# Attention with forgetting, then a SiLU feed-forward: turning the first blocks of batches four to seven with full-array products, and a new order of loads on SyncE

## The chip, the cores and the metric

The kernel runs on one core of a Trainium2 chip. The metric is the device time of one execution in microseconds (us), and less is better. TensorE (PE in the profile) multiplies matrices into PSUM, ScalarE (ACT) and VectorE (DVE) work on PSUM and SBUF, GpSimd (POOL) works on SBUF and issues DMAs, and SyncE (SP) issues DMAs. A number such as L298 is a line of the kernel before.

## The reference

Inputs are q, k, v of 8 batches x 8 heads x 576 tokens x 64, forget values f, and two weights. All are float32.

```python
scores = scale * q @ k.T                  # scale = 1/8
cum = cumsum(log(clip(f, 1e-4, 1)))
attn = softmax(where(causal, scores + cum[:, None] - cum[None, :], -1e9))
x = (attn @ v) laid out as 4608 tokens x 512
h = x @ w_in                              # 512 x 2048
out = (h * sigmoid(h)) @ w_out            # 2048 x 512
```

## The kernel before

**Tiling.** All matmuls take bf16. Each head's 576 tokens are a first block of 128, three more blocks of 128 ("the rest") and a tail of 64. The decay is split into a factor for each key, which is multiplied into v, so that the softmax needs no row maximum: exp of the scores, a mask, the product with v and a column of ones, and a division. Two heads make a pair; a unit n is one pair of one batch, b, p = divmod(n, 4), 32 units in all.

**Stages.** First come the first blocks of batches 0 to 3, in straight code (L780 to L821). Then `two_more(4, True)` (L883) and `two_more(6, False)` (L889) do the first blocks of batches 4, 5 and 6, 7. Then a loop over m (L965) takes two units at a time and computes the rest and the tails. The feed-forward runs in between: `m1_chunk` (L574) makes 128 columns of the hidden layer for a group of tokens (four matmuls into `hp`, a tanh on ACT, L589, a product on DVE, L590), and `m2_part` (L608) or `m2_rows` (L643) multiplies by `w_out`. `fill(us, least)` (L752) puts such steps between the attention's, by costs that are written in the code; it knows nothing of when a buffer is free.

**A first block.** `load_qk0(b)` (L129) brings q and k so that a partition holds eight neighbouring tokens of one head (16 such runs x 8 heads = 128 partitions), in `qkb`. The scores need them with the 64 features in the partitions. `turn0(b, i)` (L290, i = 0 for q, 1 for k) does this with matmuls against `sel` (L233): for each of the 8 tokens of a run, and for each of two sets of heads, one matmul of 128 rows x 64 columns against 64 columns, which lands in the upper or lower half of the partitions of one PSUM tile `tp` (L298). One copy of 128 x 512 then takes it to SBUF: q on ACT, k on DVE (L305). `scores0` (L322) multiplies the two (L332) and takes exp on ACT (L339), `mask0` (L346) masks on DVE where no ban was added beforehand (`ban0`, L310), `out0` (L362) multiplies by v and divides, `back0` (L395) turns the result with four products of 128 columns (L402) and copies it (L403) into the token group's tile. `two_more(b, ...)` turns q and k of batch b, puts a filling step, turns q and k of batch b + 1, puts a filling step, and goes on with the scores of the one and of the other.

**Buffers.** PSUM has two pools: `psc` (two tiles of two banks, for scores) and `pbig` (L69), four tiles of one bank each under one tag "big". `tp`, `hp`, `po`, `tx`, `dn` and `pr` all take turns in these four.

**Order.** The order on each engine is the order in the text (`manual_schedule`, L54); the framework sets the semaphores between engines from what the instructions read and write, and gives a tile a free buffer. DMAs issued on one engine wait in that engine's order too.

**Loads of the loop.** `turn(n)` (L895) casts the tail columns of unit n + 3 on POOL (`cast_qk`, L407) and issues its transposing DMA on SP (`transposes`, L437). `prepare(n)` (L900) issues the loads of later units: q and k of unit n + 4 on POOL (L160); at p = 2 the tails of batch b + 2 on SP (`load_tails`, L180); the v blocks of batch b + 1 (`load_v`, L192), on SP for batch 1 and on POOL from batch 2 on; and, at p = 2 and 3, the conversions of v on POOL (`convert_v`, L427). Now `prepare(n)` comes behind `turn(n)` (L986, L995, L1016).

Of the kernel before, what the change touches and what calls it, by code (L numbers as in the profile page):

```python
# [10 lines left out]
FP32 = mybir.dt.float32  # L11
BF16 = mybir.dt.bfloat16
P = 128
# [5 lines left out]
def kernel(  # L19
# [10 lines left out]
    nc = tc.nc  # L30

    B, H, S, D = q.shape
# [4 lines left out]
    NP = H // 2  # L37
# [7 lines left out]
    NU = B * NP  # L45
    NQ = NU // 2
    HD = D // 2
    RUN = 8
# [10 lines left out]
    qktp = ctx.enter_context(tc.tile_pool(name="qktp", bufs=4))  # L59
# [9 lines left out]
    pbig = ctx.enter_context(tc.tile_pool(name="pbig", bufs=4, space=bass.MemoryType.PSUM))  # L69
# [5 lines left out]
    sel = const.tile([P, 2, D], BF16, name="sel")  # L75
# [7 lines left out]
    kT0 = [const.tile([P, NP, P], BF16, name=f"kT0_{b}") for b in range(B)]  # L83
# [149 lines left out]
    for i in range(2):  # L233
        for g in range(2):
            nc.vector.tensor_copy(
                out=sel[:, i, :].rearrange("p (u w r) -> p u w r", u=2, w=2)[:, g, :, :],
                in_=ident_bf[:, :].rearrange("p (r u i w) -> p u i w r", u=2, i=2, w=2)[
                    :, g, i, :, :
                ],
            )  # L240

    def keep_warm(n):
# [7 lines left out]
        out=f_sb[:, :], in0=f_sb[:, :], scalar1=1e-4, scalar2=1.0, op0=ALU.max, op1=ALU.min  # L250
# [39 lines left out]
    def turn0(b, i):  # L290
        src = qk0[b]
        if i == 0:
            qT0[b] = qktp.tile([P, NP, P], BF16, name="qT0", tag="qT0", bufs=2)
        dst, evac = ((qT0[b], nc.scalar.copy), (kT0[b], nc.vector.tensor_copy))[i]
        tp = pbig.tile([P, NP, NRUN, RUN], FP32, name="tp", tag="big")
        for c in range(RUN):
            for j in range(2):
                nc.tensor.matmul(  # L298
                    tp[j * D : (j + 1) * D, :, :, c].rearrange("p a r -> p (a r)"),
                    lhsT=src[:, i, c * D : (c + 1) * D],  # L300
                    rhs=sel[:, j, :],
                    start=True,
                    stop=True,
                )
        evac(  # L305
            out=dst[:, :, :].rearrange("p a t -> p (a t)"),
            in_=tp[:, :, :, :].rearrange("p a r c -> p (a r c)"),
        )

    def ban0(b):  # L310
        sc = psc.tile([P, 2, NP, P], FP32, name="sc", tag="sc")
        for i in range(2):
            nc.tensor.matmul(  # L313
                sc[:, i, :, :].rearrange("p a t -> p (a t)"),
                lhsT=ident_bf[:, :],
                rhs=ban[:, :, :].rearrange("p a t -> p (a t)"),
                start=True,
                stop=False,
            )
        return sc  # L320
# [25 lines left out]
    def mask0(b):  # L346
        x = u0[b][:, :, :, :].rearrange("p i a t -> p (i a) t")
        nc.vector.tensor_tensor(
            out=x, in0=x, in1=tri[:, None, :].to_broadcast([P, H, P]), op=ALU.mult
        )  # L350
# [56 lines left out]
    def cast_qk(n):  # L407
        b, p = divmod(n, NP)
        if n < NP:
            qbf[n] = conv.tile([P, NX, 2 * D], BF16, name="qkb", tag="qkb")  # L410
        t2 = qbf[n]
        for i, t in enumerate(qst.pop(n) if n < NP else ()):
            c0 = i * (NR + 1)
            nc.gpsimd.tensor_copy(
                out=t2[:, c0 : c0 + NR, :].rearrange("p c x -> p (c x)"),
                in_=t[:, :, :, :].rearrange("p c h d -> p (c h d)"),
            )
        nc.gpsimd.tensor_copy(
            out=t2[:, NR, :].rearrange("s (i d) -> s i d", i=2),
            in_=tst[b].rearrange("s (u i w) d -> s u w i d", u=2, w=2)[:, p // 2, p % 2, :, :],  # L420
        )
# [15 lines left out]
    def transposes(n):  # L437
        src = qbf.pop(n)
        t = qktp.tile([P, NX, P], BF16, name="qkT", tag="qkT")
        qkT[n] = t[:, :, :].rearrange("p x c -> p (x c)")  # L440
        nc.sync.dma_start_transpose(
            out=t[:, :, :], in_=src[:, :, :].rearrange("p x c -> p (x c)")
        )
# [308 lines left out]
    def fill(us_, least=0, ends=(0, 0)):  # L752

        left = us_ + at["left"]
        kinds = plan(left)
        kinds += [0] * (least - len(kinds))
        if any(ends) and kinds:
            if 2 not in kinds:
                kinds[0] = 2
            n1, n2 = len(kinds) - kinds.count(2), kinds.count(2)  # L760
            e0 = 1 if ends[0] else 0
            e1 = 1 if ends[1] and n2 > e0 else 0
            inner = n2 - e0 - e1
            n = n1 + inner
            mid = [2 if (x + 1) * inner // n > x * inner // n else 1 for x in range(n)]
            if inner and mid[-1] == 2 and e1 and not e0:
                mid = mid[::-1]
            kinds = [2] * e0 + mid + [2] * e1
        for k in kinds:
            t = step(k)  # L770
            if t is None:
                at["left"] = 0.0
                return
            left -= t / 1000
        at["left"] = left
# [84 lines left out]

    def two_more(b, banned):
        for x in range(2):
            turn0(b + x, 0)
            turn0(b + x, 1)
            fill(0.6, 1)
        for x in range(2):
            if banned:
                scores0(b + x, ban0(b + x))
            else:
                scores0(b + x)  # L870
                mask0(b + x)
            fill(0.6 if x == 0 else 2.0 if banned else 2.8, 1 if x == 0 else 2)
        out0(b)
        fill(0.6, 1)
        out0(b + 1)
        fill(0.8, 2)
        back0(b, on_act)
        fill(0.6, 1)
        back0(b + 1, on_act)
        fill(0.6, 1)  # L880
# [14 lines left out]
    def turn(n):  # L895
        if n < NU - 3:
            cast_qk(n + 3)
            transposes(n + 3)

    def prepare(n):  # L900

        b, p = divmod(n, NP)
        if n != NP - 1 and n + 4 < NU:
            load_qk(n + 4)
        if b + 1 == B:
            return
        if p == 2 and b + 2 < B:
            load_tails(b + 2)
        if b == 0 and p >= 2 or b > 0 and p == 1:
            for c in range(NM) if b > 0 else range(2 * (p - 2), 2 * (p - 1)):  # L910
                load_v(b + 1, c)
        if n == NP - 1:
            load_qk(n + 4)
        if p >= 2:
            for c in range(2 * (p - 2), 2 * (p - 1)) if b > 0 else range(NM * (p - 2)):
                convert_v(b + 1, c)
# [48 lines left out]
    for m in range(NQ):  # L965
        n = 2 * m
        piece = 1.7 if m < 2 else 2.4
        if m == 2:
            assert at["m2"] >= M2_OF[0]
            first_pool.__exit__(None, None, None)  # L970
            gpools[0] = ctx.enter_context(tc.tile_pool(name="third", bufs=1))
            lag["g"] = 2
        if m == 4:
            lag["parts"] = 12
        goal = (spent() if m <= 4 else goal) + QUAD[m]
        rows = whole() if m > 0 and BY_DMA[m - 1] else None
        scores(n, 0)
        scores(n, 1)
        if m > 0:
            back(m - 1)  # L980
        turn(n)
        if m > 0:
            if m % 2 == 0:
                b = m // 2 - 1
                pending.append([2, [REST_OF[b]] + ([TAILS_OF[b][0]] if b == NM - 1 else [])])
        prepare(n)  # L986
        if rows:
            at["m2"] += 4
            m2_rows(*rows, 0)
            m2_fence(*rows)  # L990
            mask(n)
            scores(n, 2)
            scores(n + 1, 0)
            turn(n + 1)
            prepare(n + 1)  # L995
            m2_rows(*rows, 1)
            mask_tail(n)
            mask(n + 1)
            scores(n + 1, 1)
            scores(n + 1, 2)  # L1000
            m2_out(*rows)
            passed()
            attend(n)
            mask_tail(n + 1)
            slot(1.9, 3)
            attend(n + 1)
            slot(1.8)
            rest(goal)
            at["left"] = 0.0
            continue  # L1010
        slot(piece, 0, (1, 0))
        mask(n)
        scores(n, 2)
        scores(n + 1, 0)
        turn(n + 1)
        prepare(n + 1)  # L1016
        slot(piece, 0, (1, 0))
        mask_tail(n)
        mask(n + 1)
        scores(n + 1, 1)  # L1020
        scores(n + 1, 2)
        mask_tail(n + 1)
        slot(piece, 0, (1, 0))
        attend(n)
        attend(n + 1)
        slot(min(3.5, max(0.8, behind() - LAG)) if m > 1 else 0.8)
# [39 lines left out]
```

## Time and profile before

| | |
|---|---|
| three runs | 342.59 us median, 340.6 to 344.43 |
| the profiled execution | 340.25 us, span of its instructions 338.5 us |
| TensorE busy | 331.3 us, 4136 matmuls |
| L298, the turning matmuls | 256, from 5.5 to 48.8 us |
| L332 in the two stages of two_more | from 27.67 to 29.8 and from 49.98 to 51.25 us |
| 16 DMA engines | 52.4% of the span for POOL's queue, 43.2% for SP's |

How to read it: "busy" is the time in which an engine has work, "xN" a count of instructions, and the last figures of a group are the idle time ahead of it and who ended it. The chain of waits is followed from the last instruction backwards to what released it; its rows are start, length, engine, tile, line and count, in us. The timeline merges equal instructions; "PEld" is TensorE's load of weights, "SPq" the issue of a DMA on SP. The end of a matmul is modelled, so the start of the next is the better measure of its length.

### The profile page before, as it was taken

The numbers are of one execution on the slowest core, as the hardware profiler recorded it, in microseconds if no ns is written. First come the engines' busy times: TensorE is split into PE (matmuls) and PEld (weight loads), VectorE is DVE, ScalarE is ACT, GpSimd is POOL, SyncE is SP. The second block draws the span as 40 slices with busy tenths as digits, with TensorE's granted clock in tenths as the row PEclk, the third lists the DMA queues.
The fourth block names the chain that finished last, engine by engine and source line by source line (L and its number), as shares of the span: only waits on it lengthen the run. The fifth ranks groups of instructions, "written<-read, shape, count | busy, mean of one in ns | idle before, by whom it ended". The sixth has DMA issues, their size and how long they took to land.

```text
span 338.5 us, 10020 instructions
## 1 busy us (share of the span) xinstructions
PE 331.3 (98%) x4136; PEld 222.7 (66%) x4136; DVE 189.8 (56%) x423; ACT 216.9 (64%) x389; POOL 188.0 (56%) x269
## 2 busy tenths in 40 slices
PE   7999999999999999999999999999999999999995
PEld 3745655577656767858767796867777685555654
DVE  4665735265467458656665865675485564333330
ACT  5767735776767767848748794875877583344331
POOL 8995417893798998999995994694000000000000
PEclk9999999999999999999999999999999999999999
DMA  8999999999699999999999999896452200001012
GB/s 156 190 188 222 189 199 166 186 213 174 114 109 214 138 212 137 169 219 197 150 169 123 200 133 117 149 185 85 99 74 61 59 35 31 31 33 64 33 62 62
DMA packets 124542, 45.24 MB, mean 134 GB/s; under 512 B 111824, under 2 KB 118224, under 8 KB 124496
## 3 DMA queue, kind: packets, MB, share of 16 engines
q0 software_dynamic: 53536, 18.88, 52.4%
q1 hardware_dynamic: 70800, 25.59, 43.2%
q8 instruction: 32, 0.52, 0.7%
q10 hardware_dynamic: 160, 0.13, 0.2%
q14 instruction: 14, 0.11, 0.1%
HBM read 36.85 MB, written 9.44 MB: 137 GB/s over the span
## 4 chain that ended last, share of the span: by engine, by line
PE 93%; ACT 2%; DMA 1%; DVE 1%; issue 1%; POOL 0%; POOLq 0%
PE hp L581 36%; PE po L626 25%; PE pr L652 12%; PE sc L473 7%; PE dn L520 6%; PE dn L529 3%; PE tp L298 2%; DMA qkb<-in_k_dram 1%; PE sc L313 1%; PE sc L332 1%; DVE gt L590 1%; ACT x L403 1%; PE tx L562 1%; DVE xq L387 0%; ACT th L589 0%
## 5 line engine op out<-in xcount | busy, mean ns | idle before, releaser
L590 DVE SCALAR_TENSOR_TENSOR gt<-th,hp 128x384 bf16<-128x384 bf16 (+2 forms) x208 | 107.4, 523 | 74.6 <-ACT th L589 65.8
L589 ACT ACTIVATE th<-hp 128x384 bf16<-128x384 f32 (+2 forms) x208 | 96.5, 471 | 73.4 <-PE hp L581 71.7
L581 PE MATMUL hp<-x,w_in_bf 128*128 128x384 bf16 (+2 forms) x704 | 123.0, 321 | 0.5 <-DVE x L565 0.3
L581 PEld LDWEIGHTS <-w_in_bf 128*128 128x128 bf16 x832 | 78.9, 98 | 49.4 <-issue 1.1
L626 PE MATMUL po<-w_out_bf,gt 128*128 128x512 bf16 (+1 forms) x400 | 93.8, 371 | 0.0
L484 ACT ACTIVATE u<-sc 128x1024 bf16<-128x1024 f32 (+1 forms) x96 | 74.7, 817 | 7.0 <-PE sc L473 7.0
L626 PEld LDWEIGHTS <-gt 128*128 128x128 bf16 x400 | 37.6, 98 | 32.5 <-issue 0.2
L652 PE MATMUL pr<-w_out_bf,gt 64*128 64x256 bf16 x768 | 46.0, 269 | 0.0
L160 POOL DMA_DIRECT2D qkb<-in_q_dram x56 | 43.8, 784 | 1.8 <-issue 1.8
L160 POOL DMA_DIRECT2D qkb<-in_k_dram x56 | 43.3, 775 | 1.0 <-DMA vf<-in_v_dram 1.0
L427 POOL TENSOR_TENSOR vp<-vf,w_bf 128x520 bf16<-128x520 f32 (+1 forms) x32 | 35.2, 1106 | 12.3 <-DMA vf<-in_v_dram 11.4
L652 PEld LDWEIGHTS <-gt 64*128 64x128 bf16 x768 | 38.5, 94 | 2.8
L636 ACT ACTIVATE osb<-po 128x512 f32<-128x512 f32 (+1 forms) x25 | 14.6, 584 | 26.5 <-PE po L626 26.5
L473 PE MATMUL sc<-qkT 64*128 64x128 bf16 (+1 forms) x640 | 27.8, 206 | 0.3 <-ACT u L484 0.3
L473 PEld LDWEIGHTS <-qkT 64*128 64x128 bf16 x640 | 20.0, 94 | 8.2 <-issue 6.4
L490 DVE TENSOR_TENSOR u<-u,tri 128x768 bf16<-128x768 bf16 x32 | 19.5, 610 | 9.6 <-ACT u L484 9.6
L478 ACT ACTIVATE ut<-sc 128x640 bf16<-128x640 f32 x32 | 22.6, 708 | 1.9 <-PE sc L473 1.7
L520 PEld LDWEIGHTS <-u 128*128 128x128 bf16 x576 | 20.6, 98 | 2.9
L520 PE MATMUL dn<-vp,u 128*128 128x65 bf16 x384 | 21.8, 193 | 0.0
L538 DVE TENSOR_TENSOR xr<-dn,rec 128x448 bf16<-128x448 f32 x32 | 20.0, 624 | 1.1
L192 POOL DMA_DIRECT2D vf<-in_v_dram x24 | 20.3, 859 | 0.0
L520 PE MATMUL dn<-v,u 128*128 128x65 bf16 x192 | 20.0, 194 | 0.0
(74 smaller groups left out, 244.7 us busy)
## 6 DMA issues: line engine op xcount, KB each, us to landing
out_dram<-osb SPq DMA_DIRECT2D x32, 256.0 KB, 3.5
vf<-in_v_dram POOLq DMA_DIRECT2D x24, 256.0 KB, 6.0
qkb<-in_q_dram POOLq DMA_DIRECT2D x56, 48.0 KB, 4.5
qkb<-in_k_dram POOLq DMA_DIRECT2D x56, 48.0 KB, 4.9
vf<-in_v_dram SPq DMA_DIRECT2D x8, 256.0 KB, 5.1
w_in_bf<-in_moe_w_in_dram POOLq DMA_DIRECT2D x4, 512.0 KB, 7.2
w_out_bf<-in_moe_w_out_dram POOLq DMA_DIRECT2D x4, 512.0 KB, 8.9
qkb<-in_q_dram POOLq DMA_DIRECT2D x8, 128.0 KB, 5.5
```

Of the source, the lines that this page charges most:

```text
L160: nc.gpsimd.dma_start(out=t2[:, c0 : c0 + NR, j * D : (j + 1) * D], in_=src[b, head(p, j), P:SM, :].rearrange("(c p) d -> p c d", p=P),)
L192: q_.dma_start(out=t[r, :, 0:D], in_=v[b, :, P + c * P : min(S, P + (c + 1) * P), :].rearrange("h p d -> p h d"),)
L427: nc.gpsimd.tensor_tensor(out=vbf[b][r, c, :, :], in0=vst[b][c][r, :, :], in1=w_bf[r, c + 1, b * H : (b + 1) * H, None].to_broadcast([n, H ...
L473: nc.tensor.matmul(sc[:, i, o : o + q1 - q0], lhsT=kt, rhs=t[r, q0:q1], start=True, stop=True)
L478: nc.scalar.activation(out=ut[:, :, 0:3:2, :].rearrange("p k i t -> p i k t"), in_=sc[:, :, T0 : T0 + (NM + 1) * ST].rearrange("p i (k t) ...
L484: nc.scalar.activation(out=u[:, :, c * SM : c * SM + w], in_=sc[:, :, 0:w], func=ACT.Exp, scale=scale)
L520: nc.tensor.matmul(dn[:, i * NR + c - 1, :], lhsT=u[:, i, o : o + P], rhs=vals(kb, i), start=(kb == 0), stop=(kb == c),)
L581: nc.tensor.matmul(hp[:, :], lhsT=w_in_bf[:, cc, fc * P : (fc + 1) * P], rhs=xcols(g, cc), start=(cc == 0), stop=(cc == NCC - 1),)
L589: nc.scalar.activation(out=th[:, :], in_=hp[:, :], func=ACT.Tanh, scale=0.5)
L590: nc.vector.scalar_tensor_tensor(out=gt[:, fc, :], in0=th[:, :], scalar=1.0, in1=hp[:, :], op0=ALU.add, op1=ALU.mult,)
L626: nc.tensor.matmul(po[:, :], lhsT=gt[:, fc, tb * P : (tb + 1) * P], rhs=w_out_bf[:, fc, m0:m1], start=(fc == 0), stop=(fc == NFC - 1),)
L652: nc.tensor.matmul(pos[g, tb][y], lhsT=gt[r, fc, tb * P : (tb + 1) * P], rhs=w_out_bf[r, fc, y * DM // 2 : (y + 1) * DM // 2], start=(half ...
```

## The change

For batches 4 to 7, `flip0` takes the place of `turn0`. It multiplies two neighbouring tokens at once: 128 stationary columns (two tokens x 64 features) against both halves of `sel` (128 columns), four products for q and four for k. The result has the first token of each pair in the upper 64 partitions and the second in the lower, and both sets of heads side by side in the columns. Four copies of 64 x 256 put them right, for each token of the pair (c) one on ACT for the first set of heads (j = 0) and one on DVE for the second; each writes every second element of its half of the destination. Batches 0 to 3 keep `turn0`.

`prepare(n)` moves into `turn(n)`, between the cast and the transposing DMA, so that what it issues on SP comes ahead of that DMA. On POOL the order stays.

```diff
+    def flip0(b, i):
+        src = qk0[b]
+        if i == 0:
+            qT0[b] = qktp.tile([P, NP, P], BF16, name="qT0", tag="qT0", bufs=2)
+        dst = (qT0[b], kT0[b])[i][:, :, :].rearrange("p a t -> p (a t)")
+        tp = pbig.tile([P, RUN // 2, 2, D], FP32, name="tf", tag="big")
+        for z in range(RUN // 2):
+            nc.tensor.matmul(
+                tp[:, z, :, :].rearrange("p j x -> p (j x)"),
+                lhsT=src[:, i, z * P : (z + 1) * P],
+                rhs=sel[:, :, :].rearrange("p j x -> p (j x)"),
+                start=True,
+                stop=True,
+            )
+        for c in range(2):
+            for j, copy in enumerate((nc.scalar.copy, nc.vector.tensor_copy)):
+                copy(
+                    out=dst[j * D : (j + 1) * D, :].rearrange(
+                        "p (x z c) -> p x z c", z=RUN // 2, c=2
+                    )[:, :, :, c],
+                    in_=tp[c * D : (c + 1) * D, :, j, :].rearrange("p z x -> p x z"),
+                )
...
     def two_more(b, banned):
         for x in range(2):
-            turn0(b + x, 0)
-            turn0(b + x, 1)
+            flip0(b + x, 0)
+            flip0(b + x, 1)
             fill(0.6, 1)
...
     def turn(n):
         if n < NU - 3:
             cast_qk(n + 3)
+        prepare(n)
+        if n < NU - 3:
             transposes(n + 3)
...
         scores(n, 0)
         scores(n, 1)
         if m > 0:
             back(m - 1)
         turn(n)
...
-        prepare(n)
         if rows:
...
             turn(n + 1)
-            prepare(n + 1)
             m2_rows(*rows, 1)
...
         turn(n + 1)
-        prepare(n + 1)
         slot(piece, 0, (1, 0))
```

## The prediction

> **What bounds the kernel now.** First the page's busy times and slices, to see which engine is full and where.
>
> ```profile
> PE 331.3 (98%) x4136; PEld 222.7 (66%) x4136; DVE 189.8 (56%) x423; ACT 216.9 (64%) x389; POOL 188.0 (56%) x269
> ...
> PE   7999999999999999999999999999999999999995
> DVE  4665735265467458656665865675485564333330
> ACT  5767735776767767848748794875877583344331
> ```
>
> TensorE (PE) is full from the second slice to the last but one, so what it no longer does is gained, and every time it is made to wait is lost. Then the chain of waits in order of time, at the two stages that turn batches 4, 5 and 6, 7:
>
> ```profile
> 23.34 1.01 PE tp L298 x32
> 24.35 0.97 PE hp L581 x4
> 25.32 1.01 PE tp L298 x32
> 26.33 0.97 PE hp L581 x4
> ...
> 46.51 1.01 PE tp L298 x32
> 48.06 1.01 PE tp L298 x32
> 49.08 0.97 PE po L626 x4
> ...
> 53.52 0.86 PE po L626 x4
> ```
>
> A block is one batch's q and k: 32 matmuls, 1.01 us on the chain. The four full-array matmuls ahead of a block take 0.97 us instead of 0.86: 0.11 us goes with the change to half-width matmuls. Third, the groups by form, for prices:
>
> ```profile
> L305 DVE CAST kT<-tp 128x512 bf16<-128x512 f32 x8 | 5.5, 690 | 4.5 <-PE tp L298 4.5
> L305 ACT CAST qT<-tp 128x512 bf16<-128x512 f32 x8 | 4.7, 583 | 2.4 <-PE tp L298 2.4
> L387 DVE TENSOR_TENSOR xq<-dn,rec 128x256 bf16<-128x256 f32 x6 | 2.5, 423 | 0.2
> L403 ACT COPY x<-tx 128x256 bf16<-128x256 bf16 x1 | 0.4, 373 | 0.0
> ```
>
> Fourth, the timeline, for a full-array product of 128 columns, for the starts that I count from, and for SP's queue:
>
> ```profile
> 34.57 0.39 PE L402 MATMUL tx<-ident_bf,xq 128*128 128x128 bf16 x4
> 34.79 1.03 PE L581 MATMUL hp<-x,w_in_bf 128*128 128x512 bf16 x4
> 50.85 0.40 PE L332 MATMUL sc<-qT,kT 64*128 64x128 bf16 x8
> 72.53 2.89 SPq L441 DMA_TRANSPOSE qkT<-qkb  x2
> 75.47 0.62 SPq L180 DMA_DIRECT2D qktf<-in_q_dram  x1
> 76.81 1.99 SPq L192 DMA_DIRECT2D vf<-in_v_dram  x2
> 79.04 4.14 SPq L441 DMA_TRANSPOSE qkT<-qkb  x1
> 83.24 1.25 SPq L192 DMA_DIRECT2D vf<-in_v_dram  x2
> 83.52 2.06 POOL L427 TENSOR_TENSOR vp<-vf,w_bf 128x520 bf16<-128x520 f32 x2 [5.48 <-DMA vf<-in_v_dram]
> ```
>
> **The change part by part.**
>
> TensorE. Per block 32 half-width matmuls (1.01) and the mode change (0.11) go; 8 matmuls of 128 columns come. Four of those stand 0.22 us ahead of the next work (34.57 to 34.79), so 0.44 a block. Saved: 1.01 + 0.11 - 0.44 = 0.68, over four blocks 2.7 us. This is all that the change can give on a full TensorE, 0.8% of 340 us.
>
> Copies. Per batch one 128x512 copy on ACT (0.58) and one on DVE (0.69) go; four copies of 64x256 come on each. Copies of 64 partitions and of every second output element are not in the trace. The nearest rows, with as many elements in each partition, are 0.373 (L403, ACT) and 0.423 (L387, DVE): I take 0.38 and 0.42. From below: four L403 copies in a row take 2.05 us on the timeline, 0.51 apart at 0.59 long, so a copy behind another may count 0.08 less, 0.30 and 0.34. From above: no cheaper than the whole 128x512, 0.58 and 0.69. At my values ACT does 4 x 0.38 = 1.52 us a block instead of 0.58, DVE 1.68 instead of 0.69.
>
> Who waits for that. Per batch TensorE goes on, after one filling step, to the next batch's two products, and these need a free buffer of tag "big"; there are four, shared with hp, po and tx. A product's buffer was free one copy after it; now it is free after the last of four copies on two engines. Behind the copies on ACT stand the tanh and then the exp of scores0; behind those on DVE the product of L590, which frees the hp buffers.
>
> Whether ACT and DVE may copy out of one buffer at the same time decides the rest. No row shows it: hp is read by ACT and, after it, by DVE; where two engines share one turned batch (back0(3)) each has a tile of its own. So bounds from both sides.
>
> (a) They overlap. Second stage, us after 46.35, counting 0.15 from one engine to the next: products end at 0.22 and 0.44; ACT copies 0.37 to 1.89, DVE 0.37 to 2.05; hp's tanh and product end at 2.7; the first product of batch 7 waits for its buffer until 1.36, the second until 2.2; po ends 3.3; the last copy of batch 7 on DVE ends 4.4 and scores0(7) starts at 4.7, where it starts at 4.5 now (50.85). So +0.2. First stage the same way, with hp 512 wide (tanh 0.60, product 0.69), which holds two of the four buffers longer: +0.3. Sum +0.5: the 2.7 us that TensorE saves are spent waiting for buffers. With the lower prices the sum is -0.5, with the upper +3.7.
>
> (b) They take turns within a buffer, in the order written: ACT, DVE, ACT, DVE. From ACT to DVE the tanh and its product show 0.03 (22.25 to 22.28); back I take 0.1. One buffer's chain is 0.38 + 0.03 + 0.42 + 0.1 + 0.38 + 0.03 + 0.42 = 1.76, and the next one's first ACT copy runs beside the last DVE copy, so two buffers need 3.07 us. Second stage: chain from 0.37 to 3.44; tanh to 3.4, product to 3.86; products of batch 7 at 2.26 and 3.59; its DVE copies begin behind that product at 3.86, and the chain from there ends at 6.5; scores0(7) at 6.7 instead of 4.5: +2.2. First stage: DVE starts at 1.5 behind the product of the hp before, so the chain ends at 4.16, tanh and product at 5.03, batch 5's chain at 7.7; scores0(5) at 7.85 (31.0) instead of 6.2 (29.4): +1.6; ACT is then late by its queue of tanh and exp, and back0(5), at the end of the stage, comes 2.7 late. I take 2.1 between these. Sum +4.3; with all lower prices +3.2, with my prices and the late end +5.0, with the upper prices +10.7.
>
> I take (b): the two copies of a half read the same partitions of one buffer, and every row with two engines on one PSUM tile shows them one after the other. Later work doesn't make it good: TensorE has no idle slice in which to catch up.
>
> The Trainium skill, "PSUM — Partial Sum Buffer" (section "PSUM bank collisions raise a hardware error"), speaks against this change: two engines that touch one bank in the same 32 partitions at one time collide, reads too, so they must be ordered, by bank or by bank and quadrant. By bank the sum would be (b), +4.3; by quadrant only the two copies of one half would take turns, and the sum would be (a) and 0.1 more, +0.6. No run here shows which ordering the program gets.
>
> SP. Only tail loads and the v loads of batch 1 change places; POOL's order stays. At unit 2 the two tail loads and two v loads go ahead of a transpose: 0.62 + 0.63 + 1.99, with gaps 3.3 us in SP's queue. That transpose, issued at 74.19 and landing 4.6 us later by the median, lands at 82.1 at the latest; its scores come at 85.0 (the L473 rows of that unit). At unit 3 two v loads (1.25) pass a transpose that sat for 4.14 us on SP; they land some 4 us earlier, and POOL's idle times of 5.48 and 1.62 before L427 shrink by up to 4. Nothing on TensorE waited for those conversions, so that gives 0. From unit 6 on it is two tail loads, 1.3 us, ahead of one transpose in four; transposes are issued three units ahead, about 20 us, and TensorE never waits for qkT's DMA. I cost this at 0, covered by those 20 us; without the cover it would be 1.3 us in each of four batches, 5 us; a gain beyond 0.3 us is excluded, as that is all that PE L473 waits for a DMA.
>
> Sum: -2.7 on TensorE is already inside; net +4.3 + 0.
>
> **Own time.** The profiled execution took 340.25 us, span 338.5 and 1.75 around it. The sum gives 344.6 against it. The three runs have a median of 342.59, and the mean of all four is 342.0; against that, 346.3, which I forecast.
>
> **The rivals.** About 1% (3.4 us) is what a measurement here can tell from no change.
>
> - Copies overlap, (a), on the other side of my forecast: +0.5, 342.5. Its place is between the products of one batch and those of the next; it decides if a buffer is free within 1.7 us of its product, as the 0.68 us saved per block then pays for the wait. For it: the two halves are different partitions. Against: the two copies of one half.
> - Copies overlap but cost as much as 128x512 ones, because of the step of two elements on the output: +3.7, 345.7. Nothing in the trace has that step.
> - The copies hide and TensorE gets its 2.7 us: 339.3. For it: ACT was idle 1.86 us before batch 6's copy. Against: four buffers, two of them held by hp in the first stage.
> - Transposes late behind the tail loads: +5, 347. Against: 20 us of lead.
>
> **How the numbers follow.** Chances: turns 0.58; overlap 0.22; dear copies 0.09; hidden 0.06; transposes 0.05. The likeliest, turns, gives 346.3, with its own range from 342.0 + 3.2 = 345.2 to 350. The range of all reaches down to overlap with its lower price, 341.5, leaving out the hidden case and part of overlap; up to 350.0, leaving out the dearest copies with turns (352.7). Slower by over 1%, above 345.4 against the mean: nearly all of turns (0.55), two thirds of dear copies (0.06), transposes (0.05): 0.66. Faster needs under 339.2: part of the hidden case, 0.05. Within 1%: 0.29.
>
> **What would show it.** Right: 8 matmuls of 0.44 us a block where 32 stood; copies near 0.38 and 0.42; in the timeline ACT and DVE alternating on one tf buffer; the second product of batches 5 and 7 starting over 2.5 us after the first batch's; scores0(7) 2 us later against the block's start. Wrong: copies of ACT and DVE on one tile at the same time; copies of 0.3 or less; TensorE waiting for qkT.

## The result, and the profile after

The changed kernel takes 345.66 us (median of 16 runs, 344.8 to 348.09), the kernel before 341.76 in its 16 (340.16 to 346.95). The ratio is 1.0127, 95% interval 1.0103 to 1.015: 4.3 us slower (3.5 to 5.1). The profiled execution has a span of 343.5 us instead of 338.5. Runs that took over 1.5% longer than the fastest of their kernel are left out of the ratios here and below, so that 4.3 is not the difference of the two medians, and the profiled execution of e1 was such a one and isn't used.

TensorE's busy time is 0.4 us shorter (330.9 after 331.3) and yet the span is 5 us longer. The windows of the kernel after show where (columns: length; busy time and instruction count of PE, PEld, DVE, ACT and POOL, in this order; the granted clock, the DMA share and GB/s).

```profile
23.00:32.00 9.00, 6.52 (x52) 3.10 (x51) 6.15 (x13) 5.80 (x13) 5.61 (x10) 1.00 1.20 219
32.00:45.00 13.00, 12.57 (x93) 7.50 (x92) 9.63 (x20) 9.38 (x19) 5.04 (x8) 1.00 1.19 196
48.00:56.00 8.00, 4.68 (x44) 2.60 (x44) 4.20 (x10) 4.37 (x10) 5.32 (x10) 1.00 0.86 171
100.00:280.00 180.00, 179.94 (x2628) 131.86 (x2628) 114.58 (x254) 130.26 (x228) 117.13 (x156) 1.00 1.04 136
```

And the same windows of the kernel before.

```profile
23.00:32.00 9.00, 9.00 (x116) 4.83 (x115) 5.21 (x8) 6.48 (x11) 4.88 (x8) 1.00 1.20 221
32.00:45.00 13.00, 12.83 (x90) 7.75 (x89) 8.70 (x19) 7.79 (x18) 5.26 (x8) 1.00 1.20 206
48.00:56.00 8.00, 8.00 (x97) 4.85 (x97) 5.06 (x11) 4.44 (x8) 6.46 (x11) 1.00 0.87 171
```

TensorE, the first figure, was full in both stages of two_more. Now it stands idle for 2.5 of 9 us in the first and for 3.3 of 8 us in the second. ACT and DVE are not full there either (5.80 and 6.15 of 9; 4.37 and 4.20 of 8): no engine of the three is at its limit. Later, 100 to 280 us, TensorE is busy for 179.94 of 180 us. The clock is 1.00 throughout.

Who waits for whom is in the timeline of the second stage after (in brackets: idle time before the row, and what ended it).

```profile
49.28 0.44 ACT L326 CAST qT<-tf 64x256 bf16<-64x256 f32 x1 [1.52 <-PE tf L317]
49.76 0.44 DVE L326 CAST qT<-tf 64x256 bf16<-64x256 f32 x1 [1.54 <-ACT qT L326]
50.23 0.44 ACT L326 CAST qT<-tf 64x256 bf16<-64x256 f32 x1 [0.50 <-DVE qT L326]
50.70 0.45 DVE L326 CAST qT<-tf 64x256 bf16<-64x256 f32 x1 [0.51 <-ACT qT L326]
51.29 0.38 PE L317 MATMUL tf<-sel,qkb 128*128 128x128 bf16 x4 [1.39 <-DVE qT L326]
52.12 0.45 DVE L326 CAST kT<-tf 64x256 bf16<-64x256 f32 x1 [0.50 <-ACT kT L326]
52.72 0.38 PE L317 MATMUL tf<-sel,qkb 128*128 128x128 bf16 x4 [1.04 <-DVE kT L326]
55.46 0.23 PE L355 MATMUL sc<-qT,kT 64*128 64x128 bf16 x1 [0.63 <-ACT kT L326]
55.95 0.39 PE L355 MATMUL sc<-qT,kT 64*128 64x128 bf16 x7 [0.26 <-DVE kT L326]
```

The four copies of q's buffer run strictly one after the other, ACT, DVE, ACT, DVE, each 0.44 us, and each engine stands idle for 0.5 us while the other works. The next batch's products wait 1.39 and 1.04 us until buffers are free, and the scores of batch 7 wait for the last copies. The third copy is the telling one: it reads the lower 64 partitions (c = 1), and the copy that it waits for reads the upper 64.

### The profile page after: what moved, and what is told of

It is laid out like the page before. It is cut to its first block, busy times and chain, and to the rows that moved or that the text cites. A ratio compares the mean times of both kernels' runs of the same rounds, so it can differ in the third digit from the quotient of the medians.

```text
span 343.5 us, 9856 instructions
## 1 busy us (share of the span) xinstructions
PE 330.9 (96%) x4040; PEld 221.7 (65%) x4040; DVE 194.5 (57%) x435; ACT 220.7 (64%) x401; POOL 186.5 (54%) x269
## 4 chain that ended last, share of the span: by engine, by line
PE 87%; DVE 4%; DMA 3%; ACT 3%; issue 1%; POOL 1%; POOLq 0%
PE hp L604 34%; PE po L649 24%; PE pr L675 12%; PE sc L496 7%; PE dn L543 5%; PE dn L552 3%; DMA vf<-in_v_dram 2%; DVE gt L613 1%; DMA qkb<-in_q_dram 1%; DVE qT L326 1%; DVE kT L326 1%; ACT th L612 1%; ACT qT L326 1%; PE tx L585 1%; DVE xq L410 1%
## 5 line engine op out<-in xcount | busy, mean ns | idle before, releaser
L513 DVE TENSOR_TENSOR u<-u,tri 128x768 bf16<-128x768 bf16 x32 | 18.5, 578 | 9.4 <-ACT u L507 9.3
```

## The experiments

Each ratio is of a kernel's runs to those of the kernel before on the same chip. "Late by" is the start of the same ACT instruction in the two traces, subtracted: before the first stage (th at 20.78 us of the kernel before), after it (osb at 44.38), after the second (th at 60.15) and at the end (osb at 333.0). A trace's start differs, by up to 1 us; a stage's share is the difference of two columns.

| run | ratio, 95% interval | late by: before, after stage 1, after stage 2, end |
|---|---|---|
| the change | 1.0127 (1.0103 to 1.015) | 0.17, 2.51, 5.09, 5.02 |
| e1, turning alone | 1.012 (1.0077 to 1.0163) | not used |
| e2, order on SP alone | 0.9977 (0.9946 to 1.0008) | 0.39, 0.39, 0.39, 0.33 |
| e3, one engine a buffer | 1.0013 (0.9979 to 1.0047) | 0.15, 0.35, 0.75, 0.68 |
| e4, one engine a token | 1.0028 (0.9991 to 1.0064) | -0.19, 0.30, 1.54, 1.47 |
| e5, a buffer for each engine | 0.998 (0.9956 to 1.0004) | 1.03, 1.35, 1.95, 1.89 |
| e6, old products, four copies | 1.0094 (1.0056 to 1.0132) | 0.00, 1.77, 4.46, 4.39 |
| e7, new products, one copy | 0.997 (0.9943 to 0.9997) | 0.12, -0.47, -0.86, 0.19 |
| e8, q and k in one copy | 0.9968 (0.9939 to 0.9997) | 0.00, -0.02, -0.09, 0.45 |
| e9, copies in another order | 1.0047 (1.0026 to 1.0069) | 0.19, 1.58, 2.40, 3.07 |
| e10, as e8 with SP's old order | 0.998 (0.9952 to 1.0009) | 0.29, 0.27, 0.20, 0.28 |

In us against the kernel before, the ratios are +4.3 for the change, +4.1 for e1, -0.8 for e2, +0.4 for e3, +1.0 for e4, -0.7 for e5, +3.2 for e6, -1.0 for e7, -1.1 for e8, +1.6 for e9 and -0.7 for e10. In every row that has both, e7's apart, they lie 0.2 to 1.6 us below what the stages lose in the traces. The profiled execution of the kernel before took 340.25 us, 1.5 less than its median, which goes some way to explain it. So, of what was expected of these times, e2, e4, e5 and e6 came out below it and e7 and e9 above it, but all of their intervals except e7's reach into the expected range. Where a ratio can't tell theory and rival apart, as in e4, the trace has to.

**e1 and e2: the two parts apart.** e1 puts `prepare` back behind `turn`; e2 keeps `turn0` in `two_more`.

```diff
 # e2, against the changed kernel
-            flip0(b + x, 0)
-            flip0(b + x, 1)
+            turn0(b + x, 0)
+            turn0(b + x, 1)
```

> The new products and copies alone; SP's loads stand where they stood before. Theory (the copies of ACT and DVE out of one PSUM buffer take turns, and the stages of batches 4 to 7 end later by that): the whole loss is here, +4.3 us against the kernel before (between +3.5 and +5). Rival (part of the loss is SP's, transposes late behind the tail loads): +2 or less, and the rest in the run that has the new order alone.

> The old turning, the new order of loads on SP alone. Theory: 0, between -0.5 and +0.5 us, as TensorE waits neither for the transposed q and k nor for the conversions of v. Rival (SP's order costs): +2 us or more.

e1 has the loss, 4.1 us (2.6 to 5.6); e2 has none (1.8 us faster to 0.3 slower). That the moved loads do go out earlier is in e2's timeline on SP and POOL.

```profile
77.13 2.54 SPq L464 DMA_TRANSPOSE qkT<-qkb  x1
79.72 1.76 SPq L192 DMA_DIRECT2D vf<-in_v_dram  x2
81.72 2.36 SPq L464 DMA_TRANSPOSE qkT<-qkb  x1
...
80.29 1.04 POOL L450 TENSOR_TENSOR vp<-vf,w_bf 128x520 bf16<-128x520 f32 x1 [2.70 <-DMA vf<-in_v_dram]
83.12 1.05 POOL L450 TENSOR_TENSOR vp<-vf,w_bf 128x520 bf16<-128x520 f32 x1 [1.79 <-DMA vf<-in_v_dram]
85.44 2.44 POOL L450 TENSOR_TENSOR vp<-vf,w_bf 128x520 bf16<-128x520 f32 x2 [1.27 <-DMA vf<-in_v_dram]
```

The second pair of v loads goes out at 79.72 instead of 83.24, and POOL's waits for v fall from 7.1 us (5.48 + 1.62) to 5.8 (2.70 + 1.79 + 1.27). Yet e2's row in the table is nearly the same after this place as before it, 0.33 and 0.39: TensorE gains nothing from POOL's shorter waits.

**e3: no buffer read by two engines.** The same eight copies on each engine in a stage's batch pair, the same shapes and the same buffers; only who copies what is other.

```diff
-            for j, copy in enumerate((nc.scalar.copy, nc.vector.tensor_copy)):
+            for j, copy in enumerate([(nc.scalar.copy, nc.vector.tensor_copy)[i]] * 2):
```

> As the changed kernel, but ACT makes all four copies of q and DVE all four of k, so that no PSUM buffer is read by two engines. The number of copies on each engine, their shapes and the products stay. Theory (turns): copies stand one behind the other at 0.36 to 0.44 us, both engines at work at once, and the loss falls from +4.3 to between 0 and +1 us against the kernel before. Rival (the number of copies and their length is the cost, not the turns): still +3.5 us or more.

```profile
24.02 1.78 ACT L326 CAST qT<-tf 64x256 bf16<-64x256 f32 x4
24.76 1.81 DVE L326 CAST kT<-tf 64x256 bf16<-64x256 f32 x4
```

Each engine makes its four copies without a pause, and for most of the time both are at work. The stages lose 0.6 us instead of 4.9 (0.75 - 0.15 against 5.09 - 0.17). The number of copies and their length, 0.44 us here too, are not what costs most; the turns are.

**e5: no buffer read by two engines, one destination written by both.** Here the products are made for each set of heads by itself, q's and k's into one buffer, and ACT reads the one, DVE the other.

```diff
+            tfs[b] = [pbig.tile([P, 2, RUN // 2, D], FP32, name="tf", tag="big") for _ in range(2)]
+        for j in range(2):
+            for z in range(RUN // 2):
+                nc.tensor.matmul(
+                    tfs[b][j][:, i, z, :],
...
+                    rhs=sel[:, j, :],
```

> As the changed kernel, but the two sets of heads go to PSUM buffers of their own, which hold q and k of one batch: ACT copies out of one, DVE out of the other, with the same eight copies and the same destinations, which both engines still write. The products have 64 columns and are 32 in place of 16 a pair of tensors. Theory (the turns come from the shared PSUM buffer): no turns, between 0 and +1.2 us against the kernel before. Rival (the turns come from the shared destination in SBUF): turns stay, +3.5 us or more.

```profile
48.25 0.89 ACT L334 CAST qT<-tf 64x256 bf16<-64x256 f32 x2 [1.64 <-PE tf L321]
48.37 0.90 DVE L334 CAST qT<-tf 64x256 bf16<-64x256 f32 x2 [1.31 <-PE tf L321]
```

There are no turns, and the stages lose 0.9 us. Both engines still write halves of one SBUF tile, so the turns do not come from there.

**e4 and e6: is it the partitions or the buffer?** In e4 ACT takes the first token (upper 64 partitions) and DVE the second (lower 64).

```diff
-            for j, copy in enumerate((nc.scalar.copy, nc.vector.tensor_copy)):
+            for j, copy in enumerate([(nc.scalar.copy, nc.vector.tensor_copy)[c]] * 2):
```

> As the changed kernel, but ACT copies the first token of each pair (the upper 64 partitions of the buffer, both sets of heads) and DVE the second (the lower 64). Theory (turns by whole buffer, whichever partitions are read): DVE's first copy of a buffer waits for ACT's second, one handover a buffer in place of three, and the loss is between, +1.2 to +2.8 us. Rival (turns only where two engines read the same partitions): the two work at once, 0 to +1 us.

```profile
47.07 0.89 ACT L326 CAST qT<-tf 64x256 bf16<-64x256 f32 x2 [1.51 <-PE tf L317]
47.98 0.89 ACT L326 CAST kT<-tf 64x256 bf16<-64x256 f32 x2
47.99 0.91 DVE L326 CAST qT<-tf 64x256 bf16<-64x256 f32 x2 [1.98 <-ACT qT L326]
48.93 0.91 DVE L326 CAST kT<-tf 64x256 bf16<-64x256 f32 x2
```

In e4's timeline DVE starts on q's buffer at 47.99, when ACT's second copy of it ends (47.07 + 0.89), although it reads other partitions. While DVE works on q, ACT works on k: with one handover a buffer the engines fall into step, and the stages lose 1.7 us. The ratio alone, +1.0 us (-0.3 to +2.2), would not exclude the rival; the start at 47.99 does.

e6 is the other side: the old half-width products, with the halves right from the start, and four copies in the change's order, so that ACT reads the upper and DVE the lower partitions all the time.

```diff
+        tv = tp[:, :, :, :].rearrange("p a r (z c) -> p (a r) z c", c=2)
+        for c in range(2):
+            for j, copy in enumerate((nc.scalar.copy, nc.vector.tensor_copy)):
+                r = slice(j * D, (j + 1) * D)
...
+                    in_=tv[r, :, :, c],
```

> The old products (half-width, halves already right) with four copies of 64x256 a buffer, ACT on the upper 64 partitions and DVE on the lower 64, in the order of the changed kernel. Theory (turns by whole buffer; what TensorE saves is spent in waiting for buffers): turns stay although no partition is shared, and the time is the changed kernel's or up to 0.7 us above, +4 to +5.5 us against the kernel before. Rival (turns by partitions): +0.5 to +1.5 us. Rival (TensorE's saving is worth its full 2.7 us): +7 us.

```profile
48.89 0.44 ACT L329 CAST qT<-tf 64x256 bf16<-64x256 f32 x1 [1.86 <-PE tf L318]
49.36 0.45 DVE L329 CAST qT<-tf 64x256 bf16<-64x256 f32 x1 [1.88 <-ACT qT L329]
49.84 0.44 ACT L329 CAST qT<-tf 64x256 bf16<-64x256 f32 x1 [0.52 <-DVE qT L329]
50.31 0.45 DVE L329 CAST qT<-tf 64x256 bf16<-64x256 f32 x1 [0.50 <-ACT qT L329]
```

Turns stay, and the stages lose 4.5 us; the ratio, +3.2 (1.9 to 4.5), lies below what was expected, but its interval holds neither rival's figure. Two things follow. In these programs the order is by whole buffer, whichever partitions are read; the profile infers who released whom from the program's semaphores. And with turns TensorE's faster products are worth nothing here: e6, which has none of them, loses 4.5 where the change loses 4.9.

**e9: the same turns without the idle time.** Products, buffers and sharing as in the change; while ACT copies out of q's buffer DVE copies out of k's, then they swap.

```diff
         for c in range(2):
-            for j, copy in enumerate((nc.scalar.copy, nc.vector.tensor_copy)):
...
+            for y in range(2):
+                for j, copy in enumerate((nc.scalar.copy, nc.vector.tensor_copy)):
+                    x = y ^ j
...
```

Here `x` says which of q and k is copied.

> The same products, buffers, copies and sharing of each buffer by both engines as in the changed kernel; only the order of the eight copies of a batch is other: while ACT copies out of q's buffer DVE copies out of k's, and then they swap. Turns stay in each buffer (three handovers at 0.03 us), but no engine stands idle for the other: four steps of 0.44 + 0.03, 1.9 us a batch in place of 3.4. Theory (the loss is idle time of the engines in the turns, and lies in the order): +0.3 to +1.5 us against the kernel before. Rival (two engines on one buffer cost in themselves): +3.5 us or more.

The ratio is 1.0047, +1.6 us, just above what was expected (0.9 to 2.4 by the interval), far from the change's 4.3. The stages lose 2.2 us in its trace. A change of order alone takes more than half of the loss away; what stays above e3 is mostly that both buffers come free only at the end of four steps: the next batch's products wait for them 1.50 and 1.52 us in the two stages, in e3 0.58 and 1.22.

**e7: the products alone.** One copy of 128x512 a buffer, as before; the halves stay wrong, which is what it leaves out.

```diff
+        (nc.scalar.copy, nc.vector.tensor_copy)[i](
+            out=dst, in_=tp[:, :, :, :].rearrange("p z j x -> p (z j x)")
+        )
```

> The new products with one copy of 128x512 a buffer, q on ACT and k on DVE as before; what is left out is putting the halves right, so that scores of the first blocks of batches 4 to 7 are of wrong pairs. Theory: this is the gain that the products alone hold, -2.7 us against the kernel before (-2 to -3). Rival (the stages are bound by the copies and not by TensorE): -1 us or less.

This missed: -0.3%, 1.0 us (0.1 to 1.9) and not 2.7. By the ratio it isn't even told apart from e2 (0.997 and 0.9977), which has the old products. Its timeline has reasons, for one execution.

```profile
31.00 0.42 PE L390 MATMUL dn<-v,u 128*128 128x65 bf16 x8 [0.19 <-POOL v L371]
...
45.88 0.61 PE L317 MATMUL tf<-sel,qkb 128*128 128x128 bf16 x8
46.32 0.60 PE L599 MATMUL hp<-x,w_in_bf 128*128 128x256 bf16 x4
...
53.05 0.42 PE L390 MATMUL dn<-v,u 128*128 128x65 bf16 x8 [0.20 <-POOL v L371]
54.06 0.42 PE L390 MATMUL dn<-v,u 128*128 128x65 bf16 x8 [0.16 <-POOL v L371]
...
119.59 3.60 PE L599 MATMUL hp<-x,w_in_bf 128*128 128x384 bf16 x21 [0.95 <-DMA x<-xr]
```

One block of the four does take 0.44 us (45.88 to 46.32). The other three take 0.71, 0.60 and 0.55 (to the start of the next work): in each, a product starts 0.05 to 0.06 us after a copy or a product on DVE has ended that frees a buffer. So the exps of the two stages come 0.94 and 1.06 us earlier, 2.0 in all and not 2.7. Then the product with v waits for POOL's conversion of v, and 1.0 us is left after the second stage. In the first stage that conversion starts at 29.89, in the kernel before at 29.80, so it is a limit that was close all along; in the second it starts at 51.95, there at 50.49, so it is itself later in this execution. And the 1.0 us is lost again at 119.59, where TensorE waits 0.95 us for the transposed x from SP's DMA: here a TensorE that ran ahead ran into a transfer that came too late for it.

**e8 and e10: a version that could beat both.** As e5, with q and k of a batch side by side in SBUF too, so that one copy of 64x512 takes both; e10 has SP's old order as well.

```diff
+    kqk = [const.tile([P, 3, NP, P], BF16, name=f"kqk_{i}") for i in range(2)]
...
+                    out=kqk[b % 2][j * D : (j + 1) * D, x0 : x0 + 2, :, :].rearrange(
+                        "p i a (r z c) -> p i (a r) z c", z=RUN // 2, c=2
+                    )[:, :, :, :, c],
+                    in_=tfs[b][j][c * D : (c + 1) * D, :, :, :].rearrange("p i z x -> p i x z"),
```

> As the run with a PSUM buffer for each engine, but q and k of a batch lie side by side in SBUF too, so that one copy of 64x512 takes both: two copies a batch on each engine in place of four. Theory (no turns, and the fixed part of a copy is paid half as often: 2 x 0.65 = 1.3 us a batch and engine in place of 1.5 to 1.76): -0.3 to -1.5 us against the kernel before, the first version that may beat it. Rival (buffers are still free too late, as q's copies begin only after k's products): 0 to +1 us.

> The version with q and k of a batch in one copy, with SP's loads in the old order: is it faster than the kernel before, and is the new order of loads part of that? Theory: the stages of batches 4 to 7 gain 0.1 us in the profile of that version, and SP's order is worth nothing, so the ratio is 0.997 to 1.002 here as there. Rival (the new order on SP gains some 0.2%): 1.0 or above here.

e8's ratio is 0.9968, e10's 0.998, and both stages together are worth 0.1 us in either trace. e2, whose turning is the kernel before's, has 0.9977: these three are not told apart, and a gain of 0.1 us can't be called one. The tile page of e8 has a reason.

```profile
L333 ACT CAST kqk<-tf x8: 714/725/733, 23.9 to 49.7; 64x512 bf16<-64x512 f32 x8
L333 DVE CAST kqk<-tf x8: 719/729/740, 24.7 to 50.0; 64x512 bf16<-64x512 f32 x8
...
who waited for it (us, times):
...
  PE tf L320: 1.3, 2
```

Two copies of 0.73 us a batch stand on each engine where the kernel before has one of 0.58 or 0.69, and TensorE's next products wait 1.3 us for them, about half of the 2.7 us that the products save; the rest isn't accounted for. No version here is shown to beat the kernel before by its turning.

**e11: what a copy costs.** Batches 4 and 5 write whole runs and read in steps, 6 and 7 read and write whole runs; the order of the tokens is what is left out.

> One engine a buffer; what is left out is the order of the tokens in the turned tile: the copies of batches 4 and 5 write whole runs (input still in steps), those of 6 and 7 read and write whole runs. One look at the length of a 64x256 copy, 0.44 us in the changed kernel. If the output's step of two elements is what it costs over the rows of 128x256 (0.37 on ACT, 0.42 on DVE): 0.38 to 0.40 on ACT in all four batches. If it is the input's order: 0.44 in batches 4 and 5 and 0.38 to 0.40 in 6 and 7. If it is the half of the partitions: 0.44 in all.

```profile
L329 ACT CAST qT<-tf x8: 353/366/369, 24.0 to 27.1; 64x256 bf16<-64x256 f32 x8
L329 DVE CAST kT<-tf x8: 408/422/428, 24.7 to 28.4; 64x256 bf16<-64x256 f32 x8
L334 ACT CAST qT<-tf x8: 364/366/369, 47.0 to 50.2; 64x256 bf16<-64x256 f32 x8
L334 DVE CAST kT<-tf x8: 416/422/428, 47.2 to 50.9; 64x256 bf16<-64x256 f32 x8
```

The columns are minimum, median and maximum in ns, of one execution. The median is 366 on ACT in both stages: it is the output's step of two elements that makes 440 of it; on DVE it makes 443 of 422. The order of the input costs nothing (batches 4 and 5 against 6 and 7). Nor does half the partitions, as far as the rows of 128x256 can be compared, 373 and 423, which are of other instructions or types.

## Why the prediction was right, point by point

- **TensorE.** A block of 0.44 us instead of 1.12 was right as a price (e7: 45.88 to 46.32), though only one block of four reaches it. That the saving would be spent in waiting was right too, and e6 shows it: with turns, the stages with the new products lose no less (4.9 us) than those with the old ones (4.5).
- **Turns.** The choice of (b) over (a) was what decided, and the trace after shows the turns row by row. It was chosen on an argument about the two copies of one half, and that argument is not what decides: the runs show a stricter rule in this program, a turn for each buffer whatever its partitions (e4, e6). Turns for the copies of one half alone were priced at +0.6 by the prediction itself, so that the right choice was in part luck. By the quadrant wording of the Trainium skill ("PSUM — Partial Sum Buffer", section "PSUM bank collisions raise a hardware error") the prediction's sum would have been +0.6; the program follows the wording by bank, and the measured +4.3 decides. Whether two engines on different partitions of one bank could run at once here was not tried, since every kernel here is ordered by bank.
- **Sizes.** A copy is 0.44 us, not 0.38 and 0.42: the step on the output, which no row of the trace before has. The way back from DVE to ACT is 0.03 us (50.20 to 50.23), not 0.1. The two errors cancel in part: two buffers need 3.3 us (49.28 to 52.57) where 3.07 was worked out. The lower prices rest on a misreading: the four L403 copies in 2.05 us are three of 128x512 and one of 128x256, which start at 15.90, 16.36, 16.98 and 17.57, not 0.51 apart each.
- **Stages.** Forecast +2.1 and +2.2; measured 2.34 (0.17 to 2.51) and 2.58 (2.51 to 5.09). In the first the exps come 2.8 late (3.01 - 0.17) and 0.5 of that is made good by the end of the stage; from the end of the second the delay stays to the end (4.9 and 4.85 us more than ahead of the stages), as the full TensorE had promised. The stages thus lose 4.9 in the trace and not 4.3; that the ratio says 4.3, the forecast's own figure, is luck within its 3.5 to 5.1.
- **SP.** Costed at 0, and no cost shows in e1 and e2. The second pair of v loads goes out 3.5 us earlier (79.72 instead of 83.24), about the 4 us worked out, but POOL's waits shrink by 1.3 us in all and not by up to 4.
- **Rivals.** "Overlap" has its price matched by e3 (+0.6 in the stages against +0.5), which shares no buffer, but not its condition. "Dear copies" is true of the step, by 0.07 us on ACT, and too small to matter. The gain of "hidden", 2.7 us, is the figure that failed: e7 has no cost for halves at all and still gains only 1.0. The prediction named buffers as the only thing in the way; they take some 0.7 of the 2.7 in e7's trace, and in this one execution POOL's conversion of v takes the next 1.0.
- **Bounds.** The limit for "slower", 345.4, is 1% above the mean of 342.0, but the one for "faster", 339.2, is 1% below the median of 342.59; against the mean it would be 338.6. This touches a chance of 0.05 alone.

## What to carry to other kernels

When two engines empty one PSUM buffer, look at the order in which their reads are written: if the program hands a buffer over as a whole, as this one does, alternate copies run one after the other and both engines look half idle. Give each engine a buffer of its own, or at least write the copies so that each works on one while the other works on the next (e3, e9). And before trading products for copies on a full TensorE, take the extra copies away once (e7): with one copy a buffer the gain was 1.0 us (0.1 to 1.9) and not 2.7, because buffers and, in its trace, the next things were only just in time.

## What was not expected of the hardware

A copy out of PSUM that writes every second bf16 element is longer: 440 instead of 366 ns on ACT and 443 instead of 422 on DVE for 64x256. For 64x512 it is 725 on ACT, where the whole-run copy of 128x512 takes 583: 1.11 ns an element between 256 and 512 elements ((725 - 440) / 256), against 0.85 without the step ((583 - 366) / 256, two forms). A handover between ACT and DVE costs 0.03 to 0.04 us in both directions (49.72 to 49.76 and 50.19 to 50.23 in the kernel after).
